# A hand-written instruction order for the attention start and the first block of layer 1, in place of the scheduler's

## The chip, the core and the metric

The program runs on one core of a Trainium2 chip. The metric is the device time of one execution in microseconds: the median of 3 runs of the kernel before is 971.0 (968.24 to 971.59). The profile comes from one further execution, which took 971.32 us; its recorded span, from the first to the last instruction, is 969.6 us. All times below count from the start of that span.

The engines are named as the profile names them: PE is TensorE (matmuls, PEld its weight loads), DVE is VectorE, ACT is ScalarE, POOL is GpSimd, SP is SyncE, which only issues DMAs here. ACT issues some DMAs too.

## The reference

Linear attention with a decaying state runs over 4 batches of 768 tokens with 8 heads of 48, and its output goes through two feed-forward layers (384 to 2048 and back):

```
state = alpha[:, :, t, :, None] * state + einsum(k[:, :, t], v[:, :, t])   # per head 48 x 48
y[:, :, t] = einsum(q[:, :, t], state)
x = y as (3072 tokens, 384)
h = x @ w_in;  g = max(0.01 * h, h);              x = g @ w_out            # layer 1
h = x @ w_in2; g = where(h > 0, h, exp(h) - 1);   out = g @ w_out2         # layer 2
```

The weights arrive as 64-bit floats, which the kernel converts itself.

## The kernel before

**Attention** is cut into 24 units of 128 tokens, all 8 heads together; six units are one batch, and the state goes from one unit to the next. Per unit u the work is this (the short names are used throughout):

- *prep*, DVE: a backward product scan E, two tiny ops for its end value (pe and its reciprocal), k times E (kS, in place in the packed input), a forward scan F, q times F (qh, in place).
- *sc*, PE: the scores, 16 instructions; *pk*, PE: kS transposed; *kn*, ACT: pk copied to SBUF.
- *mask*, DVE: two ops that make A from sc; *T*, DVE: the old state times pe.
- *po*, PE: A times v (16 instructions) and then T times qh (16 more); *pu*, PE: kn times v.
- *xh*, ACT: po to the high half of layer 1's input; *xl*, DVE: the low half; *S*, DVE: the new state from pu and T.
- After xh, ACT issues the loads of unit u + 3 (pack and v).

sc, pk, po and pu share three PSUM buffers in rotation, so pu(u) takes the place of po(u - 1) and waits until xl(u - 1) has read it. After the fourth unit of a block, six DMAs issued by SP (`gather`) move a part of the rows of x into place; only then can layer 1 of that block start.

**Layers.** A block is 4 units, 512 tokens. Step (j, m) of layer 1 takes block j and slice m of 16 of the hidden width: *h*, 9 matmuls on PE into hp; then *t* (ACT, 0.01 * hp), *max* (DVE), *gh* (ACT) and *gl* (DVE), which split g into two halves; *y*, 9 matmuls on PE that add into the block's output. Every product is made as three (high times high, low times high, high times low). Layer 2 has the same form, with other elementwise work.

**Conversions.** Slice m of layer 1's weights is needed from step (0, m) on. It is loaded into one of four staging tiles (`stage1`) and converted: two passes *p* on ACT, three ops *a* on DVE that depend one on another, *hi* on ACT, and the subtraction *b* on DVE. When b(m) is written, the load of slice m + 4 follows. So during attention's first units and block 0, DVE has three kinds of work: attention, conversions, and layer 1's max and gl. From block 1 on only two are left.

**What sets the order.** The program is written in some order, and a scheduler with its own model of the durations puts each engine's instructions in the order it finds best; each engine then runs its list strictly in that order, waiting at each instruction for what it needs. In the kernel before, only the first op of each conversion pass is pinned to its place in the program (`pin`). At the start come four whole units with two, then more conversions (`PC`), then block 0, whose steps carry the pieces of units 4 to 7 (`pieces`, one of attn_pe and attn_post each) and a conversion running ahead (`PS`). The scheduler is free to take later pieces earlier, and does.

Of the kernel before, what the change touches and what calls it, by code (L numbers as in the profile page):

```python
# [8 lines left out]
F32 = mybir.dt.float32  # L9
# [10 lines left out]
def attention_two_layers_kernel(  # L20
# [101 lines left out]
    def attn_prep(u):  # L122
# [3 lines left out]
        F = at_p.tile([PR, EXT], F32, tag="F", name="F")  # L126
# [5 lines left out]
        nc.vector.tensor_tensor_scan(F[:, 0:EXT - 1], t[:, 0:EXT - 1], d1[:, 0:EXT - 1], 0.0, ALU.mult, ALU.add)  # L132
        e2 = E[:, 1:EXT].rearrange("p (g c) -> p g c", c=C + 1)
        nc.vector.tensor_mul(kS, kS, e2[:, :, 1:C + 1])
        nc.vector.tensor_mul(qh, qh, ext(F, 0)[:, :, 1:C + 1])
        st[u] = dict(kS=kS, qh=qh, pe=pe)

    def attn_S(u):
        c = u % NC
        d = st[u]  # L140
        kS, qh = d["kS"], d["qh"]
        A = at_p.tile([128, 2, NP, C], F32, tag="A", name="A")
# [5 lines left out]
        d["A"], d["sc"] = A, sc  # L148
        if c < NC - 1:
            pk = ps_a.tile([128, NP, PR], F32, tag="at", name="pk")  # L150
            for p in range(NP):
                nc.tensor.transpose(pk[:, p, :], kS[:, p, :], ident[:PR, :PR])
            d["pk"] = pk

    def attn_S_post(u):
        c = u % NC
        d = st[u]
        for j, sc in enumerate(d.pop("sc")):
            nc.vector.tensor_mul(d["A"][:, j], sc, causal.unsqueeze(1).to_broadcast([128, NP, C]))
        if c < NC - 1:  # L160
# [3 lines left out]
        if c > 0:  # L164
            T = at_p.tile([PR, NP, D], F32, tag="cT", name="T")
            nc.vector.tensor_mul(T, st["S"], d["pe"].to_broadcast([PR, NP, D]))
            d["T"] = T

    def attn_V(u):
        c = u % NC  # L170
        d = st[u]
        vt = vts.pop(u)
# [13 lines left out]
        d["po"] = po  # L186
        if c < NC - 1:
# [9 lines left out]
    def attn_V_post(u, xh, xl, off):  # L197
        c = u % NC
        d = st.pop(u)
        po = d["po"]  # L200
        nc.scalar.copy(xh[0:PR, :, off:off + C], po)
        nc.vector.tensor_sub(xl[0:PR, :, off:off + C], po, xh[0:PR, :, off:off + C].bitcast(F32))
        if c < NC - 1:
            pu = d["pu"]
            Sn = at_p.tile([PR, NP, D], F32, tag="S", name="S")
            if c > 0:
                nc.vector.tensor_add(Sn, pu, d["T"])
            else:
# [11 lines left out]
    pinned = [False]  # L220

    def pin(ins):
        if pinned[0]:
            tc.keep_in_program_order(ins)

    def convert_p(raw, tp, ts, hi, lo):
        words = raw.rearrange("p (f t) -> p f t", t=2)
        rest = raw.bitcast(U16).rearrange("p (f t) -> p f t", t=4)[:, :, 1]
        pin(nc.scalar.activation(tp.bitcast(F32), words[:, :, 1].bitcast(F32), ACTF.Copy, scale=2.0 ** -112))
        nc.scalar.activation(words[:, :, 0], rest, ACTF.Copy, scale=2.0 ** -13)  # L230

# [27 lines left out]

    def ffn1_g(j, m):  # L260
        n = xt[j][2]
        hp = steps[1, j, m]
        t = g_p.tile([128, n], F32, tag="t", name="t")
        nc.scalar.activation(t, hp, ACTF.Copy, scale=0.01)  # L264
        nc.vector.tensor_max(t, t, hp)  # L265
        gh = gs_p.tile([128, n], F32R, tag="gh", name="gh")
        gl = gs_p.tile([128, n], F32R, tag="gl", name="gl")
        split(gh, gl, t, nc.scalar, nc.vector)
        steps[1, j, m] = gh, gl
# [303 lines left out]

    with ExitStack():
# [15 lines left out]
        LA = 2  # L590

        def conv_to(upto):
            pinned[0] = True
            for i in range(conv1.done[1], min(upto, len(order1))):
                conv1.a(i + 1)
                conv1.b(i + 1)
            pinned[0] = False

        attn_prep(0)
        for u in range(4):  # L600
            attn_pe(u, 0)
            attn_post(u, 1)
            attn_post(u, 0)
            attn_pe(u, 2)
            attn_post(u, 2)
            conv_to(PC[u] // 2)
# [9 lines left out]

        pieces = [(u, i) for u in range(4, NU) for i in range(4)]
        conv_to(LA)
        for s in range(LA):
            pe_h(seq[s])  # L620
            post_h(seq[s])
        for s, e in enumerate(seq):
            ph, j, m = e
            n = seq[s + LA] if s + LA < len(seq) else None
            now = []
            if ph == 1 and pieces:
# [34 lines left out]
            if ph == 2 and m >= KF - 10 and m % 2 == 0:  # L661
# [93 lines left out]
```

## Time and profile before

| what | value |
|---|---|
| median of 3 runs | 971.0 us |
| profiled execution | 971.32 us, span 969.6 us |
| PE busy | 929.8 us (96%), 5234 instructions |
| DVE busy | 529.4 us (55%) |
| ACT busy | 445.8 us (46%) |
| DMA | 62.38 MB, 64 GB/s on average, 243 GB/s in the first fortieth of the span |

The busy share is an average over unlike stages. From about 200 us on PE is never idle; DVE is the full engine between about 100 and 160 us, where attention, conversions and layer 1 come together; in the first 60 us no engine is full and DMA is at its busiest. A matmul counts as busy from its start to its modelled end, so a PE that is always busy may still do its work at half pace: there its instructions are longer.

### The profile page before, as it was taken

The page shows a single profiled execution, that of the slowest core. Times are in us where ns is not written, and L with a number is a line of the kernel's source. Part 1 is how long each engine was busy: PE and PEld are TensorE (multiplying, and loading weights), DVE is VectorE, ACT ScalarE, POOL GpSimd, SP SyncE. Part 2 cuts the span into 40 slices and gives each one's busy share as a digit, 9 for nine tenths or more (in the row PEclk, how much of TensorE's full clock was granted, in tenths as well). Part 3 has the DMA queues.
Part 4 walks back from the last instruction along what each step waited for, and adds up shares of the span by engine and source line. Part 5 has one row for each costly group of instructions (what it writes and reads, how often), then busy time and mean ns, then how long its engine had stood idle before and what let it go on. Part 6 is the DMA issues. An engine that isn't in the chain of part 4 may idle for free.

```text
span 969.6 us, 13094 instructions
## 1 busy us (share of the span) xinstructions
PE 929.8 (96%) x5234; PEld 781.8 (81%) x5234; DVE 529.4 (55%) x876; ACT 445.8 (46%) x783; POOL 1.1 (0%) x8
## 2 busy tenths in 40 slices
PE   4679999999999999999999999999999999999996
PEld 3557667887888788788878889999999999999995
DVE  6788998534555557454469983433433333333332
ACT  1344545322322323233367795574664744744442
POOL 0000000000000000000000000000000000000000
PEclk9969999999999999999999999999999999999998
DMA  9655561102111221211234330020100200100001
GB/s 243 184 152 160 153 181 45 29 13 58 42 41 41 58 71 53 58 41 50 58 96 141 115 98 10 1 81 1 62 20 1 72 10 1 62 0 1 33 1 37
DMA packets 25093, 62.38 MB, mean 64 GB/s; under 512 B 3936, under 2 KB 7008, under 8 KB 25024
## 3 DMA queue, kind: packets, MB, share of 16 engines
q1 hardware_dynamic: 19184, 40.54, 15.1%
q10 hardware_dynamic: 5840, 20.92, 7.5%
q8 instruction: 43, 0.70, 0.3%
q14 instruction: 26, 0.21, 0.1%
HBM read 54.37 MB, written 4.72 MB: 61 GB/s over the span
## 4 chain that ended last, share of the span: by engine, by line
PE 79%; DVE 8%; DMA 8%; ACT 2%; issue 1%; SPq 1%; DVEq 0%; ACTq 0%
PE hp L310 20%; PE hp L256 16%; PE y L281 15%; PE o L341 10%; PE oa L341 10%; DMA x2t<-in_w_dram 3%; DMA pack<-in_seqs_dram 2%; PE po L178 2%; DMA stg<-in_w_dram 2%; PE sc L147 2%; PE po L184 2%; DMA x<-x 1%; DVE x2t L235 1%; DVE t L265 1%; DVE gl L81 1%
## 5 line engine op out<-in xcount | busy, mean ns | idle before, releaser
L256 PE MATMUL hp<-x,w 128*128 128x512 f32 x864 | 218.6, 395 | 4.1 <-DMA x<-x 2.7
L310 PE MATMUL hp<-x,w 128*128 128x512 f32 x864 | 215.4, 393 | 0.0
L81 DVE TENSOR_TENSOR gl<-t,gh 128x512 fp32r<-128x512 f32 x192 | 132.7, 691 | 126.3 <-ACT gh L78 122.4
L78 ACT CAST gh<-t 128x512 fp32r<-128x512 f32 x192 | 119.0, 620 | 174.1 <-PE y L281 63.9
L256 PEld LDWEIGHTS hp<-x,w 128*128 128x128 f32 x864 | 160.4, 188 | 41.2 <-issue 3.2
L310 PEld LDWEIGHTS hp<-x,w 128*128 128x128 f32 x864 | 160.7, 188 | 29.3
L281 PE MATMUL y<-gh,w 128*128 128x512 f32 x576 | 173.2, 397 | 1.6 <-ACT gh L78 1.6
L319 DVE SCALAR_TENSOR_TENSOR t<-t,hp 128x512 f32<-128x512 f32 x96 | 66.0, 687 | 148.8 <-ACT t L318 148.8
L281 PEld LDWEIGHTS y<-gh,w 128*128 128x128 f32 x576 | 105.5, 188 | 25.6 <-ACT gh L78 3.0
L265 DVE TENSOR_TENSOR t<-t,hp 128x512 f32<-128x512 f32 x96 | 65.4, 683 | 73.8 <-ACT t L264 73.7
L281 PE MATMUL y<-gl,w 128*128 128x512 f32 x288 | 105.3, 394 | 0.0
L317 ACT ACTIVATE t<-hp 128x512 f32<-128x512 f32 x96 | 57.1, 595 | 103.7 <-PE hp L310 103.6
L264 ACT ACTIVATE t<-hp 128x512 f32<-128x512 f32 x96 | 56.8, 594 | 99.2 <-PE hp L256 99.2
L341 PE MATMUL oa<-w,gh 128*128 128x384 f32 x384 | 96.7, 337 | 0.0
L341 PE MATMUL o<-w,gh 128*128 128x384 f32 x384 | 94.7, 337 | 0.2 <-ACT x2t L292 0.2
L341 PEld LDWEIGHTS o<-w,gh 128*128 128x128 f32 x384 | 70.5, 188 | 6.0 <-ACT x2t L292 0.5
L341 PEld LDWEIGHTS oa<-w,gh 128*128 128x128 f32 x384 | 70.2, 188 | 2.9
L281 PEld LDWEIGHTS y<-gl,w 128*128 128x128 f32 x288 | 53.5, 188 | 12.1 <-issue 0.7
L341 PE MATMUL oa<-w,gl 128*128 128x384 f32 x192 | 63.0, 337 | 0.0
L318 ACT ACTIVATE t<-t 128x512 f32<-128x512 f32 x96 | 60.8, 633 | 2.3
L341 PE MATMUL o<-w,gl 128*128 128x384 f32 x192 | 61.0, 336 | 0.0
L147 PEld LDWEIGHTS sc<-pack 48*128 48x128 f32 x384 | 32.0, 210 | 20.3 <-issue 9.3
(89 smaller groups left out, 761.5 us busy)
## 6 DMA issues: line engine op xcount, KB each, us to landing
pack<-in_seqs_dram ACTq DMA_DIRECT2D x21, 674.2 KB, 4.8
stg<-in_w_dram SPq DMA_DIRECT2D x28, 384.0 KB, 3.4
x2t<-in_w_dram SPq DMA_DIRECT2D x20, 384.0 KB, 4.3
vt<-in_vals_dram ACTq DMA_DIRECT2D x21, 288.0 KB, 3.0
span<-in_seqs_dram SPq DMA_DIRECT2D x24, 226.2 KB, 2.7
x2t<-in_w_dram SPq DMA_DIRECT2D x32, 144.0 KB, 3.6
out_dram<-osb SPq DMA_DIRECT2D x24, 192.0 KB, 2.1
x<-x SPq DMA_DIRECT2D x36, 64.0 KB, 4.4
```

The costliest lines, as they stand in the source:

```text
L78: nc.scalar.copy(dst, src)
L81: (lo_engine or nc.vector).tensor_sub(lo, src, dst.bitcast(F32))
L147: nc.tensor.matmul(sc[j][:, p], lhsT=kS[r, p, :], rhs=qh[r, p, :], start=True, stop=True)
L256: nc.tensor.matmul(hp, lhsT=a[:, kk, :], rhs=x[:, kk, :n], start=(i == 0), stop=(i == 3 * KD - 1))
L264: nc.scalar.activation(t, hp, ACTF.Copy, scale=0.01)
L265: nc.vector.tensor_max(t, t, hp)
L281: nc.tensor.matmul(ytiles[j][c], lhsT=a[:, c * 128:(c + 1) * 128], rhs=x, start=(m == 0 and i == 0), stop=(m == KF - 1 and i == 2),)
L310: nc.tensor.matmul(hp, lhsT=a[:, kk, :], rhs=x[:, kk, :], start=(i == 0), stop=(i == 3 * KD - 1))
L317: nc.scalar.activation(t, hp, ACTF.Relu, scale=-1.0)
L318: nc.scalar.activation(t, t, ACTF.Exp, scale=-1.0)
L319: nc.vector.scalar_tensor_tensor(out=t, in0=t, scalar=-1.0, in1=hp, op0=ALU.add, op1=ALU.max)
L341: nc.tensor.matmul(otiles[j][i], lhsT=a[:, i * 128:(i + 1) * 128], rhs=x, start=(m == 0 and n == 0), stop=(m == KF - 1 and n == 2),)
```

## The change

Every function of a unit is split into its single operations, and these are written in a new order. `quarter(u, i)` holds unit u's second half together with unit u + 1's first half:

```diff
+        def quarter(u, i, chain=True):
+            if i == 0:
+                attn_pu(u)
+                prep_k(u + 1)
+                attn_T(u)
+            elif i == 1:
+                attn_mask(u)
+                if chain:
+                    attn_pk(u + 1)
+                    attn_kn(u + 1)
+                attn_po(u)
+            elif i == 2:
+                prep_F(u + 1)
+                attn_state(u)
+                prep_q(u + 1)
+                if chain:
+                    attn_sc(u + 1)
+                attn_xh(u, xh, off)
+                next_load(u + 3)
+            else:
+                attn_xl(u, xh, xl, off)
...
+                    gather(t, blocks[j][1] * C)
```

Conversions 0 to 2 and the first two steps of layer 1 are placed by hand between the quarters of units 2 to 4, and block 0's loop places one conversion and at most one quarter per step:

```diff
+        for u in range(UB):
+            for i in range(3):
+                quarter(u, i)
+            if u > 1:
+                conv1.a(u - 1)
+            quarter(u, 3)
+            if u > 1:
+                conv1.b(u - 1)
+            if u > 0:
+                conv1.p(u)
...
+            if s < KF:
+                ffn1_y(j, m)
+                pe_h(n)
+                ffn1_t(n[1], n[2])
+                conv1.a(s + 4)
+                if s < KF - LA:
+                    for p in quarters[13 * s // (KF - LA):13 * (s + 1) // (KF - LA)]:
+                        quarter(*p, chain=p[0] + 1 < UB + blocks[1][1])
+                ffn1_max(n[1], n[2])
+                ffn1_gh(n[1], n[2])
+                conv1.b(s + 4)
+                ffn1_gl(n[1], n[2])
+                conv1.p(s + 5)
+                in_order()
+                continue
```

`in_order` ties every instruction up to there to the one before it on its engine, so that the scheduler keeps the written order; `behind` ties all later instructions behind the last of these, and the rest of the program is scheduled as before:

```diff
+    def in_order():
...
+            if i >= traced[0] and y is not None:
+                tc.add_manual_dep(
+                    x, y.name,
+                    mybir.DependencyInfo(mybir.DependencyClass.NoSync, mybir.DependencyReason.DATA),
+                    reason="in_order")
...
-    pinned = [False]
-
-    def pin(ins):
-        if pinned[0]:
-            tc.keep_in_program_order(ins)
```

The first loads are reordered on SP's queue:

```diff
         constants()
+        load_unit(1)
         load_v(0)
-        load_unit(1)
+        load_unit(2)
+        load_v(1)
         stage1(0)
-        load_v(1)
-        stage1(1)
-        load_unit(2)
         load_v(2)
-        stage1(2)
-        stage1(3)
+        for m in range(1, 4):
+            stage1(m)
```

What this makes of DVE's list in unit 2, where the first conversion stands. Before, from unit 2's second mask (L159) on; L128 to L135 are the prep of unit 3, L234, L235, L237 and L241 are conversion 0 (a, a, a, b), L202 is xl(2):

```order
L159 TENSOR_TENSOR A<-sc_253,causal 128x512
L130 TENSOR_SCALAR pe<-E 112x4
L134 TENSOR_TENSOR pack<-pack,E 112x512
L131 RECIPROCAL d_97<-pe 112x4
L132 SCALAR_TENSOR_TENSOR F<-pack,d_97 112x516
L207 TENSOR_TENSOR S<-pu,T 112x192
L234 TENSOR_SCALAR x2t_138<-x2t_134 128x768
L135 TENSOR_TENSOR pack<-pack,F 112x512
L235 SCALAR_TENSOR_TENSOR x2t_138<-x2t_138 128x768
L166 TENSOR_TENSOR T<-S,pe 112x192
L237 ISA x2t_138<-x2t_134,x2t_138 128x1536
L202 TENSOR_TENSOR x<-po,x 112x4x128
```

And now (L180 mask of unit 2, L139 and L144 the rest of prep 3, L248 S, L275 to L278 conversion 0's a, L240 xl(2), L282 its b):

```order
L180 TENSOR_TENSOR A<-sc_317,causal 128x512
L180 TENSOR_TENSOR A<-sc_318,causal 128x512
L139 SCALAR_TENSOR_TENSOR F<-pack,d_97 112x516
L248 TENSOR_TENSOR S<-pu,T 112x192
L144 TENSOR_TENSOR pack<-pack,F 112x512
L275 TENSOR_SCALAR x2t_138<-x2t_134 128x768
L276 SCALAR_TENSOR_TENSOR x2t_138<-x2t_138 128x768
L278 ISA x2t_138<-x2t_134,x2t_138 128x1536
L240 TENSOR_TENSOR x<-po,x 112x4x128
L282 TENSOR_TENSOR w_0_103<-x2t_138,w_0_102 128x768
```

The two masks now stand together, and conversion 0's three dependent ops stand one right behind the other, where before an op of the attention stood between each two.

On PE, at the start of layer 1. Before, from the first matmul of unit 4's po on: one matmul of h(0, 0) and one of h(0, 1) (L256) stand inside unit 4's attention:

```order
L152 MATMUL pk<-ident,pack 128x112 x4
L178 MATMUL po<-A,vt 64x128
L256 MATMUL hp<-x,w_0_102 128x512
L256 MATMUL hp<-x,w_1_104 128x512
L192 MATMUL pu<-vt,kn 64x48
```

And now, from the end of unit 4's pu on (L231): all of h(0, 0) (L297), then unit 4's po (L212):

```order
L231 MATMUL pu<-vt,kn 48x48
L297 MATMUL hp<-x,w_0_102 128x512 x3
L297 MATMUL hp<-x,w_0_103 128x512 x3
L297 MATMUL hp<-x,w_0_102 128x512 x3
L212 MATMUL po<-A,vt 64x128
```

The steps of layer 1 are whole now, and h(0, 0) stands ahead of unit 4's po.

In block 0's loop, DVE's list for step s = 2 (a of conversion 5, the prep of unit 6 and T, max of step 4, b of conversion 5, gl of step 4):

```order
L275 TENSOR_SCALAR x2t_139<-x2t_135 128x768
L276 SCALAR_TENSOR_TENSOR x2t_139<-x2t_139 128x768
L278 ISA x2t_139<-x2t_135,x2t_139 128x1536
L127 SCALAR_TENSOR_TENSOR E<-pack,d_96 112x517
L129 TENSOR_SCALAR pe<-E 112x4
L130 RECIPROCAL d_97<-pe 112x4
L132 TENSOR_TENSOR pack<-pack,E 112x512
L187 TENSOR_TENSOR T<-S,pe 112x192
L308 TENSOR_TENSOR t<-t,hp 128x512
L282 TENSOR_TENSOR w_5_113<-x2t_139,w_5_112 128x768
L318 TENSOR_TENSOR gl<-t,gh 128x512
```

Every one of the steps s = 0 to 12 has this form, with another quarter, or none, in the middle; before, two conversions at a time were open in this stretch and mixed with two units' attention.

## Rows read from the trace of the kernel before

**Rows 1.** Windows: stretch, its length, busy us (instructions) by engine, PE clock, DMA.
```profile
0.00:61.00 61.00, 34.59 (x278) 27.84 (x278) 46.24 (x78) 17.29 (x23) 1.08 (x8) 0.88 0.75 199
74.20:177.80 103.60, 100.43 (x632) 74.38 (x633) 91.04 (x142) 50.04 (x77) 0.00 (x0) 1.00 0.46 129
177.80:250.00 72.20, 72.20 (x369) 57.92 (x370) 33.06 (x53) 21.50 (x36) 0.00 (x0) 1.00 0.09 24
```

**Rows 2.** Waits of PE: waiting line, releaser, us in total, times, longest.
```profile
PE po L178 <- DVE A L159: 9.5, 7, 2.7
...
PE pk L152 <- DVE x L202: 6.0, 4, 2.8
```

**Rows 3.** Windows of line L147 (sc) alone, up to 177.8 us.
```profile
0.00:177.80 177.80, 21.68 (x176) 18.21 (x176) 0.94 0.57 157
```

**Rows 4.** Windows of line L256 (h of layer 1) alone, up to 177.8 us.
```profile
0.00:177.80 177.80, 46.90 (x171) 30.96 (x171) 0.94 0.57 157
```

**Rows 5.** Timeline of PE: start, length, line, operation [idle before, releaser].
```profile
8.88 2.08 PE L147 MATMUL sc<-pack 48*128 48x128 f32 x16 [8.88 <-DVE pack L135]
...
40.84 1.95 PE L184 MATMUL po<-pack,T 48*48 48x128 f32 x16
...
42.71 1.19 PE L147 MATMUL sc<-pack 48*128 48x128 f32 x16
...
61.19 1.19 PE L256 MATMUL hp<-x,w 128*128 128x512 f32 x2 [1.88 <-DMA x<-x]
...
97.20 0.55 PE L152 MATMUL pk<-ident,pack 112*128 112x112 f32 x4
...
102.35 0.67 PE L192 MATMUL pu<-vt,kn 128*64 128x48 f32 x16
...
200.79 2.20 PE L256 MATMUL hp<-x,w 128*128 128x512 f32 x9
...
204.87 2.20 PE L256 MATMUL hp<-x,w 128*128 128x512 f32 x9
...
229.25 1.09 PE L178 MATMUL po<-A,vt 128*64 128x128 f32 x16
230.27 1.08 PE L184 MATMUL po<-pack,T 48*48 48x128 f32 x16
```

**Rows 6.** Timeline of DVE.
```profile
55.56 0.69 DVE L202 TENSOR_TENSOR x<-po,x 112x512 fp32r<-112x512 f32 x1
...
87.05 0.56 DVE L234 TENSOR_SCALAR x2t<-x2t 128x768 int32<-128x768 int32 x1
87.71 0.96 DVE L235 SCALAR_TENSOR_TENSOR x2t<-x2t 128x768 int32<-128x768 int32 x1
88.71 0.96 DVE L237 CUSTOM_DVE_ANT_0 x2t<-x2t,x2t 128x1536 uint16<-128x1536 uint16 x1
...
124.00 1.24 DVE L128 TENSOR_TENSOR_SCAN E<-pack,d 112x517 f32<-112x517 f32 x1
...
128.78 0.55 DVE L234 TENSOR_SCALAR x2t<-x2t 128x768 int32<-128x768 int32 x1
...
132.65 0.35 DVE L166 TENSOR_TENSOR T<-S,pe 112x192 f32<-112x192 f32 x1
132.92 0.95 DVE L237 CUSTOM_DVE_ANT_0 x2t<-x2t,x2t 128x1536 uint16<-128x1536 uint16 x1
133.78 0.68 DVE L265 TENSOR_TENSOR t<-t,hp 128x512 f32<-128x512 f32 x1
134.38 0.69 DVE L135 TENSOR_TENSOR pack<-pack,F 112x512 f32<-112x512 f32 x1
```

**Rows 7.** Timeline of ACT.
```profile
12.29 1.28 ACT L230 ACT_TABLE_LOAD   x1 [12.29 <-DMA x2t<-in_w_dram]
...
54.10 0.58 ACT L201 CAST x<-po 112x512 fp32r<-112x512 f32 x1 [0.59 <-PE po L184]
```

**Rows 8.** Chain of waits in order of time: start, length, what.
```profile
15.30 9.64 DMA pack<-in_seqs_dram
```

More of the change, by code (lines that the diff above doesn't have):

```diff
@@ L186, in attn_V, with attn_pu @@
         d["po"] = po
+    def attn_pu(u):
+        c = u % NC
+        d = st[u]
+        vt = vts[u]
         if c < NC - 1:
@@ L258, in ffn1_h, with ffn1_t, ffn1_max, ffn1_gh @@
         steps[1, j, m] = hp
-    def ffn1_g(j, m):
[L261 to L269, printed above, removed]
+    def ffn1_t(j, m):
+        t = g_p.tile([128, xt[j][2]], F32, tag="t", name="t")
+        nc.scalar.activation(t, steps[1, j, m], ACTF.Copy, scale=0.01)
+        steps[1, j, m] = t, steps[1, j, m]
+    def ffn1_max(j, m):
+        t, hp = steps[1, j, m]
+        nc.vector.tensor_max(t, t, hp)
+    def ffn1_gh(j, m):
+        gh = gs_p.tile([128, xt[j][2]], F32R, tag="gh", name="gh")
+        nc.scalar.copy(gh, steps[1, j, m][0])
+        steps[1, j, m] = steps[1, j, m][0], gh
+    def ffn1_gl(j, m):
+        t, gh = steps[1, j, m]
+        gl = gs_p.tile([128, xt[j][2]], F32R, tag="gl", name="gl")
+        nc.vector.tensor_sub(gl, t, gh.bitcast(F32))
+        steps[1, j, m] = gh, gl
+    def ffn1_g(j, m):
+        for f in (ffn1_t, ffn1_max, ffn1_gh, ffn1_gl):
+            f(j, m)
     ytiles = {}
@@ L572, in general, with behind @@
                 ffn2_y(j, m)
+    traced = [0]
+    def in_order():
+        ins = list(nc.cur_bb.bb.instructions)
+        last = {}
+        for i, x in enumerate(ins):
+            y = last.get(x.engine)
+            if i >= traced[0] and y is not None:
[3 more added lines that the diff above has]
+                    reason="in_order")
+            last[x.engine] = x
+        traced[0] = len(ins)
+    def behind():
+        ins = list(nc.cur_bb.bb.instructions)
+        last = {x.engine: x for x in ins[:traced[0]]}
+        for x in ins[traced[0]:]:
+            if x.engine in last:
+                tc.add_manual_dep(
+                    x, last[x.engine].name,
+                    mybir.DependencyInfo(mybir.DependencyClass.NoSync, mybir.DependencyReason.DATA),
+                    reason="behind")
     with ExitStack():
@@ L590, in attention_two_layers_kernel @@
         LA = 2
[L592 to L597, printed above, removed]
-        attn_prep(0)
[L600 to L606, printed above, removed]
+        UB = blocks[0][1]
+        def quarter(u, i, chain=True):
+            j = unit_block[u]
+            xh, xl, _, t = xtile(j)
+            off = (u - blocks[j][0]) * C
+            if i == 0:
+                attn_pu(u)
+                prep_k(u + 1)
+                attn_T(u)
+            elif i == 1:
+                attn_mask(u)
+                if chain:
+                    attn_pk(u + 1)
+                    attn_kn(u + 1)
+                attn_po(u)
+            elif i == 2:
+                prep_F(u + 1)
+                attn_state(u)
+                prep_q(u + 1)
+                if chain:
+                    attn_sc(u + 1)
+                attn_xh(u, xh, off)
+                next_load(u + 3)
+            else:
+                attn_xl(u, xh, xl, off)
+                st.pop(u)
+                if u == blocks[j][0] + blocks[j][1] - 1:
+                    gather(t, blocks[j][1] * C)
+        attn_prep(0)
+        attn_sc(0)
+        attn_pk(0)
+        attn_kn(0)
+        for u in range(UB):
[8 more added lines that the diff above has]
+                conv1.p(u)
+        conv1.a(UB - 1)
+        quarter(UB, 0)
+        ffn1_h(0, 0)
+        ffn1_t(0, 0)
+        quarter(UB, 1)
+        conv1.b(UB - 1)
+        ffn1_max(0, 0)
+        ffn1_gh(0, 0)
+        quarter(UB, 2)
+        ffn1_h(0, 1)
+        ffn1_t(0, 1)
+        ffn1_gl(0, 0)
+        conv1.p(UB)
+        ffn1_max(0, 1)
+        ffn1_gh(0, 1)
+        ffn1_gl(0, 1)
+        in_order()
         seq = [(1, j, m) for j in range(NB) for m in range(KF)]
@@ L615, in post_h @@
             (ffn1_g if e[0] == 1 else ffn2_g)(e[1], e[2])
[L617 to L621, printed above, removed]
+        quarters = [(u, i) for u in range(UB, UB + blocks[1][1]) for i in range(4)][3:]
+        pieces = [(u, i) for u in range(UB + blocks[1][1], NU) for i in range(4)]
         for s, e in enumerate(seq):
@@ L668, in attention_two_layers_kernel @@
                     guard()
+        behind()
         with tc.If(nc.values_load(near, min_val=0, max_val=1) == 0):
```

83 lines of the change are left out of this document (52 added, 31 removed).

## The prediction

> **What bounds the kernel now.** I read the windows by stage first. In the last of the three stretches shown PE is busy for all of its 72.2 us [rows 1]; from there on the end moves with PE's work, and 969.6 - 177.8 = 791.8 us of span follow. In the first 61 us neither PE (34.6) nor DVE (46.2) is full; from 74.2 to 177.8 PE is busy for 100.4 of 103.6 [rows 1]. The waits of PE come next: po for the masks 9.5 us, pk for xl 6.0 us (its PSUM place) [rows 2]. [...] So the yardstick is: what had PE done by a given time, and what does the rest cost at full pace. By 177.8 us sc of 176 / 16 = 11 units was done [rows 3], seven more than the four that block 0 needs, and 171 matmuls of h [rows 4].
>
> **The change, part by part.** It adds and removes no arithmetic; it moves it. Three terms decide: when block 0's loop starts, how long DVE needs for it, and how much less attention is done by its end.
>
> Prices on DVE, start to next start (or length less the overlap of 0.08 that max shows, 0.68 long and followed after 0.60) [rows 6]: a scan 1.15, an op on 512 columns (mask, kS, qh, xl, max, gl) 0.60, T or S 0.27, a conversion's ops 0.47, 0.87, 0.87, and b 0.87 like L237, which has the same columns. pe and its reciprocal I put at 0.1 each, an estimate below T's 0.27. A unit is 2 x 1.15 + 5 x 0.60 + 2 x 0.27 + 0.2 = 6.0.
>
> The hand order puts dependent ops back to back. Where that happens before, L234 to L235 takes 0.66 and L235 to L237 1.00 [rows 6]; a conversion then costs 0.66 + 1.00 + 0.87 + 0.87 = 3.40, not 3.08. [...]
>
> *To the loop.* sc(0) starts at 8.88 us [rows 5]. DVE's work from there to the loop: preps of units 1 to 5, 5 x 3.7 = 18.5; masks of units 0 to 4, 6.0; nine of S and T, 2.4; xl of 0 to 3, 2.4; conversions 0 to 2, 10.2; max and gl of two steps, 2.4. Sum 41.9, so without a wait 50.8. Waits, with PE at full pace or at half:
> - Unit 0: the table load (1.28 [rows 7]) stands ahead of the first kn, since ACT's list begins with it and it took its successor's wait before. pu(0), pk(1) and po(0) queue behind kn(0), and behind them S(0) and xl(0) on DVE, all at half pace: I walk 1.6 + 2.9 = 4.5.
> - Unit 1: after the masks DVE has F, S and qh, 2.0 us; xl(1) waits for the rest of pk 0.5, po and T 2.0 or 4.1, xh 0.58 [rows 5, 7] and three hops of about 0.07: 1.3 or 3.4.
> - Units 2 and 3: a conversion's a (2.5) fills that gap, and hi stands behind xh and two DMA issues on ACT: 0.4 or 3.5 for both.
> - The end: behind qh(5) come sc(5) 1.1, h(0, 1) 2.04 and t (about 0.6, as xh), less gl's 0.6: 3.2; then gh(0, 1) stands behind two conversion passes on ACT: 1.2 more, or 1.7.
>
> Full pace 10.6, so 61.4; half 16.3, so 67.1. The first unit is at half pace and the long stretches po, T, sc can raise the clock as they did at 42.71 [rows 5]; I take the middle, 64.3. Loads hide this only if pack(3) lands: before it took 9.64 us from its issue [rows 8]; issued at about 18.8 (behind xh(0)) it lands at 28.4, about when E(3) comes up. The gather's six DMAs end 61.19 - 56.25 = 4.9 us after xl [rows 5, 6]; conversion 2 and the prep of unit 5 cover that on DVE.
>
> *The loop*, steps 0 to 12 on DVE: 13 x (3.40 + 1.20) = 59.8; attention 17.6 (xl(4) 0.6, units 5 and 6 5.8 each, unit 7 without xl 5.4): 77.4. PE has 13 steps of 204.87 - 200.79 = 4.08, 53.0, and some 11 us of attention [rows 5]: 64, so DVE is the bound and PE waits. Waits of DVE: after b, h's last six matmuls (1.5), t and hops make 2.2, gl and the next a 3.1, so nothing in a plain step. After a mask, PE's po and T (2.15 with hops), y and h (4.08), t and hops (0.8) make 7.0 to the next max, while DVE has max, b, gl, a, F, S and qh, 6.6; after a qh, sc in place of po and T makes 5.9 against DVE's 5.2 (max, b, gl, a, xl). Twice each, with hi's 0.45 in step 0: 3 us. The loads of the staged weights follow b by SP three steps ahead of their p, some 18 us against the 9.64 of the slowest landing shown [rows 8], and cost nothing unless they land twice as late; then ACT's p, and DVE's a behind it, wait for the rest. Step 13 starts at 64.3 + 77.4 + 3 = 144.7. xl(7) 0.6, gather 4.9, then h(1, 0), y(0, 15) and h(1, 1) of 2.04 each: 156.3. PE idles some 3 us of that for the gather, with nothing else in its list to fill it.
>
> *What is owed.* At that point units 0 to 7 are done and 18 steps of h (162 matmuls); the kernel before had by 177.8 units 8, 9 and 10 as well. Each is sc 1.1, pk 0.55, po 1.02, T 1.0, pu 0.67 = 4.35 [rows 5], 13.0 in all, and 9 matmuls of 4.08 / 18 = 0.227, 2.0: 15.0 us.
>
> Sum: 156.3 + 15.0 + 791.8 = 963.1 of span. The profiled execution lies 1.7 above its span (971.3 to 969.6): 964.8, say **965**. That execution is 0.3 above the median of 971.0, so it stands for it. From block 1 on the order is the scheduler's again, and PE is full in both; I cost that at nothing, and at up to 1 us for each idle gap it leaves.
>
> Bounds, by the same steps: low, full pace, conversions at 3.08 and no wait in the loop: 61.4 + 73.2 = 134.6, then 146.2, and 954.7 at the end. High, 67.1 and a wait of 1 us in each of 13 steps: 157.5, then 169.1, and 977.6. The sum stands between them, nearer the low one because the quarters give DVE something to do while PE catches up.
>
> **The rivals.**
> - *B, DVE never waits.* The low bound, 955. For it: half pace gives way to full after the long stretch po, T, sc at 42.71 [rows 5], and conversions cover units 2 and 3. [...] Against: PE at half pace for most of 8.88 to 42.
> - *C, the round trip sets the step: slower.* Place: block 0's loop, where max(s + 2) stands in DVE's list behind h(s + 2), which needs b(s + 2) of the step before, and two passes on ACT stand ahead of t. I leave 0.9 us of slack in a plain step. If the true trip is longer than DVE's work between, everything behind max waits, 13 times. From 0.5 us a step (13 x 0.5 = 6.5) the gain is gone; at 1 us to 1.2 us it is 978 to 980. For it: PE at half pace would need 1.4 more for the six matmuls alone, and no other work of DVE may pass max now. Against: a quarter stands in twelve of the 13 steps, and PE is at full pace in the like stretch before (clock 1.00) [rows 1].
> - *D, the gain is eaten.* Half pace to the loop (2.8 later) and packs late by some 3.5 us, since all the staged weights share the DMA engines with pack(3): 971, no change. For it: DMA landing took 9.64 [rows 8]; against: packs 1 and 2 now go ahead of the weights.
> - *That the order is not what it says* is excluded: the listing shows DVE and PE in the written order.
>
> **How the numbers follow.** My forecast (960 to 970) 0.50, B 0.20, D 0.14, C 0.16. What a measurement can tell from no change is 0.5%, so faster means below 966.1 and slower above 975.9. Faster: 0.29 of the forecast's 0.50 and all of B, 0.20, with 0.01 of D: 0.50. Slower: C but for 0.01, 0.15. Same: 0.35. The range, 954 to 977, takes in B's and most of C's time and leaves about 0.2 outside.
>
> **What would show it.** Right: y(0, 0) starts at 58 to 64 us, when before h(0, 0) had only begun (61.19 [rows 5]); from there to about 144 DVE is busy nearly throughout and PE is not; dependent conversion ops start 0.66 and 1.00 apart; an idle PE of 2 to 3 us before h(1, 0), released by the gather; block 1 takes about 83 us (16 x 4.08 + 4 x 4.35), not the 72 of before. Wrong: PE's rows at full pace from unit 1 on (B); DVE idle ahead of max in every step (C); E(3) or p released by a DMA (D); idle gaps of PE after block 0.

## The result, and the profile after

The changed kernel takes 976.8 us (median of 5 runs, 975.9 to 979.5) against 971.0: 1.0072 times the time before, 95% interval 1.005 to 1.0095. It is slower by 0.7%, where 965, a gain, was forecast; it lies just inside the stated range of 954 to 977, near the time of rival C. Its profiled execution took 976.15, span 974.4 us.

The windows of the changed kernel, columns as in [rows 1]:

```profile
0.00:61.00 61.00, 34.42 (x317) 27.20 (x317) 43.88 (x76) 14.27 (x20) 1.14 (x8) 0.78 0.83 209
...
0.00:75.00 75.00, 46.68 (x390) 36.67 (x391) 52.46 (x88) 21.17 (x31) 1.14 (x8) 0.82 0.73 188
...
70.00:155.84 85.84, 72.76 (x386) 55.15 (x385) 76.80 (x110) 47.57 (x68) 0.00 (x0) 0.92 0.39 113
...
74.20:177.80 103.60, 88.93 (x458) 67.60 (x458) 83.70 (x123) 52.73 (x78) 0.00 (x0) 0.92 0.38 107
177.80:250.00 72.20, 72.20 (x485) 57.50 (x484) 44.93 (x74) 19.17 (x32) 0.00 (x0) 1.00 0.22 61
```

In the stretch from 74.2 to 177.8, where PE was busy for 100.4 us at a granted clock of 1.00 [rows 1], it is now busy for 88.9 at 0.92. From 177.8 on it is full, as before. A window of the kernel before, to set beside the second row, and its first y:

```profile
0.00:75.00 75.00, 48.40 (x370) 37.84 (x371) 58.21 (x98) 24.96 (x35) 1.08 (x8) 0.86 0.73 195
...
74.48 1.52 PE L281 MATMUL y<-gh,w 128*128 128x512 f32 x6
```

By 75 us DVE, which the forecast had as the bound of the loop, had worked 58.2 us before and has worked 52.5 now. The first y comes 8.0 us earlier (66.49, before 74.48), but with 3 conversions behind it instead of 4 and the three ops a of a fifth. So far the earlier y is DVE work put off, not saved.

PE's timeline after (start, length, line, operation, idle before and releaser); L158 is sc, L166 pk, L212 and L218 po and T, L297 h, L335 y:

```profile
33.23 1.01 PE L166 MATMUL pk<-ident,pack 112*128 112x112 f32 x4 [4.64 <-DVE A L180]
...
54.95 4.77 PE L297 MATMUL hp<-x,w 128*128 128x512 f32 x9 [5.15 <-DMA x<-x]
...
66.49 0.62 PE L335 MATMUL y<-gh,w 128*128 128x512 f32 x2
...
86.87 2.09 PE L297 MATMUL hp<-x,w 128*128 128x512 f32 x6 [2.05 <-DVE w L282]
88.75 0.95 PE L166 MATMUL pk<-ident,pack 112*128 112x112 f32 x4
90.79 2.45 PE L212 MATMUL po<-A,vt 128*64 128x128 f32 x16 [1.09 <-DVE A L180]
...
159.68 0.47 PE L297 MATMUL hp<-x,w 128*128 128x512 f32 x1 [0.68 <-DMA x<-x]
160.99 0.47 PE L297 MATMUL hp<-x,w 128*128 128x512 f32 x1 [0.84 <-DMA x<-x]
162.21 2.66 PE L297 MATMUL hp<-x,w 128*128 128x512 f32 x7 [0.76 <-DMA x<-x]
...
167.55 2.21 PE L297 MATMUL hp<-x,w 128*128 128x512 f32 x9
```

Three places lose time. h(0, 0) waits 5.15 us for the gather and then runs at half pace (4.77 for nine matmuls that take 2.2 at 167.55; the granted clock is 0.50 there and 1.00 at 167.55). In the loop PE waits for b (2.05 at 86.87), and the next pk and po run at about half pace (0.95 and 2.45, in [rows 5] 0.55 and 1.09; granted clock 0.50 from 88.75 to 93.2). At the edge to block 1 h(1, 0) dribbles, released piece by piece by the gather.

DVE's timeline after:

```profile
26.23 0.69 DVE L240 TENSOR_TENSOR x<-po,x 112x512 fp32r<-112x512 f32 x1 [2.92 <-ACT x L237]
30.08 1.23 DVE L127 TENSOR_TENSOR_SCAN E<-pack,d 112x517 f32<-112x517 f32 x1 [3.15 <-DMA pack<-in_seqs_dram]
...
60.38 0.69 DVE L308 TENSOR_TENSOR t<-t,hp 128x512 f32<-128x512 f32 x1 [2.95 <-ACT t L303]
...
67.32 0.69 DVE L308 TENSOR_TENSOR t<-t,hp 128x512 f32<-128x512 f32 x1 [3.65 <-ACT t L303]
69.39 0.69 DVE L318 TENSOR_TENSOR gl<-t,gh 128x512 fp32r<-128x512 f32 x1 [1.39 <-ACT gh L312]
70.00 0.55 DVE L275 TENSOR_SCALAR x2t<-x2t 128x768 int32<-128x768 int32 x1
...
80.21 0.56 DVE L275 TENSOR_SCALAR x2t<-x2t 128x768 int32<-128x768 int32 x1
80.87 0.96 DVE L276 SCALAR_TENSOR_TENSOR x2t<-x2t 128x768 int32<-128x768 int32 x1
81.97 0.96 DVE L278 CUSTOM_DVE_ANT_0 x2t<-x2t,x2t 128x1536 uint16<-128x1536 uint16 x1
...
99.96 0.69 DVE L308 TENSOR_TENSOR t<-t,hp 128x512 f32<-128x512 f32 x1 [2.15 <-ACT t L303]
```

The loop's first DVE op stands at 70.00. ACT's timeline after; L237 is xh(0), L111 issues pack(3), L173 is kn(1), and the last two rows begin the copies that close blocks 0 and 1:

```profile
16.41 0.58 ACT L237 CAST x<-po 112x512 fp32r<-112x512 f32 x1 [1.31 <-PE po L212]
21.88 0.32 ACTq L111 DMA_DIRECT2D pack<-in_seqs_dram  x1
...
22.88 0.53 ACT L173 COPY kn<-pk 128x448 f32<-128x448 f32 x1 [5.88 <-DMA x2t<-in_w_dram]
...
167.75 0.59 ACT L346 COPY x2t<-y 128x512 f32<-128x512 f32 x1 [0.38 <-PE y L335]
...
254.79 0.58 ACT L346 COPY x2t<-y 128x512 f32<-128x512 f32 x1 [0.68 <-PE y L335]
```

ACT stands for 5.88 us, DMA issues within, before kn(1); 4.9 of it lie between the end of xh(0), 16.99, and the issue. E(3) on DVE then waits 3.15 us for that pack. Block 1 takes 87.0 us, before 71.7 (176.09 to 247.82).

### The profile page after: what moved, and what is told of

The parts are those of the page before. It is cut to its first block, busy times and chain, and to the rows that moved or that the text cites. A ratio compares the mean times of both kernels' runs of the same rounds, so it can differ in the third digit from the quotient of the medians.

```text
span 974.4 us, 13128 instructions
## 1 busy us (share of the span) xinstructions
PE 922.9 (95%) x5234; PEld 779.2 (80%) x5234; DVE 532.4 (55%) x876; ACT 445.9 (46%) x783; POOL 1.1 (0%) x8
## 4 chain that ended last, share of the span: by engine, by line
PE 84%; DVE 6%; DMA 6%; issue 1%; SPq 1%; ACT 1%; DVEq 0%; ACTq 0%
PE hp L364 21%; PE y L335 18%; PE hp L297 18%; PE oa L395 10%; PE o L395 10%; DMA x2t<-in_w_dram 2%; PE sc L158 2%; PE po L212 2%; PE po L218 2%; DMA vt<-in_vals_dram 2%; DVE x2t L276 1%; DVE x2t L278 1%; DMA pack<-in_seqs_dram 1%; DMA x<-x 1%; DVE x2t L275 1%
## 5 line engine op out<-in xcount | busy, mean ns | idle before, releaser
L297 PE MATMUL hp<-x,w 128*128 128x512 f32 x864 | 219.6, 397 | 14.8 <-DMA x<-x 7.4
L297 PEld LDWEIGHTS hp<-x,w 128*128 128x128 f32 x864 | 162.2, 190 | 54.3 <-DVE w L282 8.0
L335 PE MATMUL y<-gh,w 128*128 128x512 f32 x576 | 179.8, 400 | 0.0
L335 PEld LDWEIGHTS y<-gh,w 128*128 128x128 f32 x576 | 106.9, 191 | 23.5 <-issue 1.1
L335 PE MATMUL y<-gl,w 128*128 128x512 f32 x288 | 109.9, 395 | 0.0
L335 PEld LDWEIGHTS y<-gl,w 128*128 128x128 f32 x288 | 54.5, 189 | 12.1
```

What stands on the lines that cost most here:

```text
L297: nc.tensor.matmul(hp, lhsT=a[:, kk, :], rhs=x[:, kk, :n], start=(i == 0), stop=(i == 3 * KD - 1))
L335: nc.tensor.matmul(ytiles[j][c], lhsT=a[:, c * 128:(c + 1) * 128], rhs=x, start=(m == 0 and i == 0), stop=(m == KF - 1 and i == 2),)
```

## The experiments

A time in brackets is the range of a kernel's runs, a ratio its time over the kernel before's with its 95% interval. The kernel before ran anew beside each group of experiments, with medians of 971.0 to 972.4; so medians of two groups can differ by 1.4 us without any change. "First y" and "block 0 ends" (start of the last row of its copies to x2t, which can hold two copies) are from the profiled execution. For the changed kernel they are 66.49 and 167.75.

**Which half loses?** loop_free drops the tie in the loop, start_free the tie of the start (`traced[0]` is set there, and nothing is tied).

```diff
                 conv1.p(s + 5)
-                in_order()          # loop_free
...
         ffn1_gl(0, 1)
-        in_order()                  # start_free
+        traced[0] = len(list(nc.cur_bb.bb.instructions))
```

> The hand order holds up to the first two steps of layer 1; block 0's loop is written as before in the same program order, but the scheduler may rearrange it. Theory 1 (the loop's order costs: the quarter stands ahead of max and b in DVE's list, so PE starves for b, drops to its lower clock and DVE then waits for PE): the loss is gone and the earlier start of layer 1 remains (first y at 66.5 us against 74.5 before), so 963 to 968 us. Rival, theory 2 (the start costs: half pace of PE and late loads before the loop): the loop is DVE-bound in either order, so no better than 972 to 977.

978.7 (977.0 to 980.8), ratio 1.0077 (1.0048 to 1.0106); first y 66.34, block 0 ends 184.18. Here the loop is left to the scheduler and only the start is by hand: slower than the kernel before, so the first theory fell. By 75 us this kernel has as many E (7), xl (5) and matmuls of h (27) as the kernel before, but 3 conversions and a part of two more, where the kernel before is at the last op of its fifth. Its DVE has worked 53.1 us by then, before 58.2. Up to there the hand-made start saves DVE nothing.

> The opposite part alone: the scheduler orders everything before block 0's loop, the loop keeps the hand order. Theory 1: the start was the part that gained, so this is as slow as the changed kernel or slower, 977 to 985 us. Theory 2: the start was the part that lost, so 966 to 972.

984.4 (982.2 to 987.8), ratio 1.0142 (1.0112 to 1.0171); first y 72.69. This is the first theory's time: for the new program the hand order of the start is worth 7.6 us. Where the scheduler orders it, E waits for packs:

```profile
DVE E L127 <- DMA pack<-in_seqs_dram: 10.7, 3, 5.0
```

So neither half alone is the one that loses: with either given back to the scheduler the new program is no faster than the changed kernel. No run gave it both halves, so what the new program and its order of the first loads cost apart from the ties is not shown.

**The gather and b.** early_gather puts one quarter into each of the first 13 steps, so that the last, and the gather behind it, come a step earlier. late_quarters puts a quarter's DVE ops behind gl and its PE and ACT ops into the next step, behind h and ahead of t.

```diff
-                    for p in quarters[13 * s // (KF - LA):13 * (s + 1) // (KF - LA)]:
+                    for p in quarters[s:s + 1]:        # early_gather
```

> Hand order throughout, but each quarter of block 0 one step earlier (steps 0 to 12 instead of 1 to 13), so that xl(7) and the gather for block 1 come a step earlier. If the edge of the blocks costs what the trace shows there (PE idle or in single matmuls between 159 and 162 us, about 2.3 us), 974 to 975 us. Theory 1 alone (waits inside the loop): no more than 1 us from 976.8, since the same quarters still stand ahead of max and b.

972.1 (970.7 to 974.3), ratio 1.001 (0.9995 to 1.0025): 4.7 below the changed kernel by the medians, more than expected, and 2.0 by the spans of the profiled executions (972.4 and 974.4). Block 0 ends at 165.14. PE's timeline at the edge:

```profile
160.75 2.48 PE L297 MATMUL hp<-x,w 128*128 128x512 f32 x9
165.11 2.20 PE L297 MATMUL hp<-x,w 128*128 128x512 f32 x9
```

h(1, 0) no longer waits, and h(1, 1) starts 2.4 earlier than at 167.55.

> Hand order throughout, same quarters in the same steps, but in each step DVE has a, max, b, gl first and the quarter's ops last, and PE's and ACT's part of a quarter stands in the next step behind h. Theory 1: PE no longer waits for b behind a prep or a mask (5.8 us of such waits in the changed kernel), stays at full pace through the loop, and DVE's waits for t go; the loop is 5 to 8 us shorter: 968 to 972 us. Theory 2: nothing before the loop changes, so 975 to 977.

979.2 (977.2 to 979.8), ratio 1.0079 (1.0055 to 1.0102). PE's waits for b are gone, but 10.3 us of waits for hi came in their place, since the quarter's copies now stand ahead of t and hi on ACT; and the gather came later (h(1, 0) waits 4.43 at 159.22). It mixed two things and settled nothing on b.

**On the round trip or off it.** Both kernels have one quarter a step, its DVE ops behind b; in the program quarter_lag has its PE and ACT ops at the head of the next step, ahead of y, quarter_behind_b right there. On PE both give the same order (h, pk, po, T, y, h), which is also that of early_gather.

```diff
+                if late:
+                    quarter_pe(*late.pop())            # quarter_lag
                 ffn1_y(j, m)
                 pe_h(n)
...
                 conv1.b(s + 4)
+                    for p in quarters[s:s + 1]:
+                        quarter_dve(*p)                # quarter_behind_b: quarter(*p)
```

> One quarter in each of the first thirteen steps, as in early_gather; its DVE ops stand behind b, and its PE and ACT ops (pu, pk, po, sc, kn, xh) stand at the head of the next step, ahead of y and so of t and hi. Theory R (the round trip b, h, t, max, b sets the loop, and the quarter ahead of b lengthens it): PE's waits for b (6.1 in early_gather) and those for the masks in the loop go, DVE's waits for t there fall below 8, first y stays at 66.2, block 0's last x2t copy starts at 160 to 163 (165.1 in early_gather), the time is 967 to 970. Rival W (DVE is near its work already; the waits only change place): other waits of the same sum appear, block 0 ends at 164 to 167, time 971 to 975.

1003.2 (1000.2 to 1003.9), ratio 1.0322 (1.0285 to 1.036). The expectation failed by 35 us, with the sign wrong. PE and DVE, one after the other:

```profile
86.73 2.45 PE L212 MATMUL po<-A,vt 128*64 128x128 f32 x16 [5.43 <-DVE A L180]
...
94.99 2.35 PE L297 MATMUL hp<-x,w 128*128 128x512 f32 x9
...
98.01 0.69 DVE L308 TENSOR_TENSOR t<-t,hp 128x512 f32<-128x512 f32 x1 [7.60 <-ACT t L303]
```

po waits for the mask (behind b) and stands ahead of y and h, so po, T, y and h all lie between this b and the next max, po, T and y at half pace (granted clock 0.50 from 86.7 to 95). From b (85.03) to max (98.01) it takes 13.0 us, with little for DVE to do. From 60 to 185 us DVE waits 35.4 us for t, in early_gather 18.6. There the mask stands ahead of max and b, so PE does po while DVE does max, b and gl, and F and qh stand ahead of the next max: from b (86.32) to max (94.64) 8.3 us. That is C's mechanism at its full price.

> As early_gather, but with the whole quarter (its PE and ACT ops too) behind b and ahead of gl. Theory R: PE's waits for b go, but PE now stands at the end of its step for masks and qh that come later on DVE, so the waits for A rise by about what those for b lose; 970 to 974. Rival (only the place of b counts): 967 to 970, block 0 ends at 160 to 163.

1000.9 (998.2 to 1002.3), ratio 1.0292 (1.025 to 1.0334): DVE waits 34.5 us for t, by the same mechanism. Both theories fell; what decides is whether po, waiting for a mask behind b, stands on PE ahead of the next y and h.

**Loads.** loads_in_turn issues packs 3 to 6 on SP instead of ACT, with the staged weights 1 to 3 behind packs 3 to 5. packs_on_pool issues only those packs and their v from POOL and leaves the weights where they were.

```diff
-        for m in range(1, 4):
-            stage1(m)
...
+            if u < 3:
+                stage1(u + 1)                          # behind quarter(u, 2)
...
-            load_unit(u, eng=nc.scalar)
+            load_unit(u, eng=nc.sync if u < 7 else nc.scalar)   # load_v too; packs_on_pool: nc.gpsimd
```

> The changed kernel with the loads of the first units in the order of use: packs 3 to 6 and their vt on the SP queue instead of ACT's, and the staged weights 1, 2 and 3 behind pack 3, 4 and 5 on it. Theory L (ACT's list stood for DMA issues and the pack came late because the weights were ahead of it): DVE's 3.15 us for pack(3) and ACT's 5.9 ahead of kn(1) go, first y comes 3 to 4 us earlier, 62 to 64, time 972 to 974. Rival (16 DMA engines are busy 0.83 of the first 61 us anyway: the weights then come late instead): p and a wait by as much, first y at 66 to 67, time 976 to 978.

970.7 (969.0 to 973.1), ratio 0.9994 (0.9975 to 1.0014): 6.1 below the changed kernel. First y 64.14. Pack(3)'s issue and E(3):

```profile
12.14 0.33 SPq L111 DMA_DIRECT2D pack<-in_seqs_dram  x1
...
27.14 1.23 DVE L127 TENSOR_TENSOR_SCAN E<-pack,d 112x517 f32<-112x517 f32 x1
```

> Packs 3 to 6 and their vt issued from POOL's list, the weights as in the changed kernel. Tells the two halves of loads_in_turn apart. If ACT's list standing at the DMA issue was the cost: kn(1) starts at 21 to 22 instead of 22.88 and pack(3) is issued at 16.5 to 18 instead of 21.9, E(3) waits under 1, first y 64 to 65, time 971 to 973. If the weights ahead of the pack in the DMA engines were the cost: pack(3) takes longer from issue to landing (over 10 us), E(3) still waits 2 to 3, time 975 to 977.

973.5 (969.3 to 974.8), ratio 1.0009 (0.9995 to 1.0023); first y 64.06, block 0 ends 162.01.

```profile
12.35 0.67 POOL L111 DMA_DIRECT2D pack<-in_seqs_dram  x1 [10.46 <-PE pk L166]
...
27.05 1.23 DVE L127 TENSOR_TENSOR_SCAN E<-pack,d 112x517 f32<-112x517 f32 x1
```

The pack's buffer is free at 12.1 to 12.4. ACT issued the load 9.5 us later, behind xh(0) and a stand that the profile puts down to a load of weights. With the weights' loads untouched E(3)'s wait is gone too, and packs 3 to 5 land 7.9 us after their issue by the median, in the changed kernel 8.2; so the late issue from ACT's list is the cause of the wait, not the bytes ahead of the pack. Most of it is the stand: issued at 16.99, when xh(0) was done, and landing 8.2 later, by an estimate at 25.2, the pack would have been there before E(3)'s turn at 26.93. Why ACT stood is not shown; in fill_pe_wide below xh(0) ended at 19.17 and the pack was issued at 21.72 all the same. The medians leave up to 2.8 us that the weights' later place may add; the two profiles don't show it, and the intervals of the two ratios overlap.

**Both.** loads_and_gather is these two edits together, loads_in_turn's and early_gather's.

> The two edits that gained, together: loads in the order of use (loads_in_turn) and the quarters one step earlier each (early_gather). If the changed kernel loses at two separate places, at its loads before the loop and at the gather behind it, the gains add: 976.8 - 6.1 - 4.7 = 966, 965 to 968. If both save the same late half pace or the same wait (early_gather also moved the rest of the loop), less than 2 us come on top: 969 to 971.

966.2 (964.8 to 969.1), ratio 0.9943 (0.9926 to 0.996): the gains add, 976.8 - 6.1 - 4.7 = 966.0. That it fits to 0.2 us is chance: by the ratios the two gains are 0.8% and 0.6%, both together 1.3%. This is faster than both kernels. First y 63.80, block 0 ends 159.25.

**b once more, with the loads in turn.** lag_behind_hi is late_quarters with the loads in turn, the quarter's ACT ops behind t and hi, and one quarter a step (its PE ops stand behind h, as there); lag_two has two quarters in its first step.

```diff
                 conv1.a(s + 4)
...
+                if late:
+                    quarter_pe(*late.pop())            # lag_two: all of late
...
                 ffn1_gl(n[1], n[2])
+                    for p in quarters[s:s + 1]:        # lag_two: quarters[s + (s > 0):s + 2]
+                        quarter_dve(*p)
+                        late.append(p)
```

> loads_in_turn, one quarter a step, with a quarter's DVE ops at the end of its step and its PE ops behind h of the next, its ACT ops behind hi there (late_quarters had them ahead of t and hi; quarter_lag had the PE ops ahead of y). Theory R' (what counts is that nothing of a quarter stands on the trip b, y, h, t, max): no waits of PE for masks or b in the loop, DVE's waits for t below 6 there, block 0's last x2t copy at 157 to 160, time 962 to 966. Rival (the chain of quarters itself, mask to pk, kn, pu, T, gets one step longer each and the gather later): no better than loads_and_gather, 967 to 974, PE waiting for sc's qh or for the gather at the edge.

970.4 (969.4 to 972.8), ratio 0.9985 (0.9972 to 0.9997): the rival. PE waits for hi (11.5 us), and for the gather at the edge (2.4).

> lag_behind_hi with two quarters in its first step, so that the last quarter, and the gather behind it, come one step earlier. If lag_behind_hi lost its gain at the edge only (its PE idled 149 to 160 for hi and the gather): block 0's last x2t copy starts at 157 to 160 (162.8 there) and the time is 964 to 967, at or below loads_and_gather's 966.2. If the loop itself is no shorter because DVE has its work there anyway: 968 to 971, with PE's waits for hi (11.5) still there.

967.5 (965.5 to 967.8), ratio 0.9954 (0.9936 to 0.9971). The time lies between the two forecasts. The gather's wait at the edge is gone, and about 3 us with it. The loop itself, first y to the end of block 0, is 161.01 - 64.97 = 96.0 us, in loads_and_gather 95.5. PE's wait has only changed its name:

```profile
PE hp L297 <- ACT w L279: 13.2, 8, 3.4
```

In loads_and_gather PE waits 6.0 us for b and 4.1 for masks. From 75 to 150 us DVE works 68.5 us here and 68.2 there. So taking the quarter from ahead of b gained nothing: DVE has its work there, and PE waits for it under one name or another. Whether it would gain with hi in time, no run shows.

**PE's pace.** Three kernels fill PE's gaps before the loop with products of a constant that nothing uses.

```diff
+                nc.tensor.matmul(wps, lhsT=d0[:, 0:128].bitcast(F32R), rhs=d0[:, 0:512].bitcast(F32R), start=True, stop=True)
...                                   # fill_pe: f32, rhs=d0[:, 128:192]
+                if i == 0:
+                    warm((0, 5, 10, 10)[u])            # all_three; and warm(16) ahead of ffn1_h(0, 0)
```

> The changed kernel with matmuls added that compute nothing of use (128x64 products of a constant into a PSUM tile that y uses later): 24 ahead of sc(0), 12 behind each pu of units 0 to 3, 30 behind pu(4), where PE stands idle. Theory P (PE's half pace is what delays DVE up to the loop): granted clock in 8.8 to 55 rises from 0.76 to over 0.9, po and T of units 1 and 2 take 1.0 to 1.1 instead of 1.95, DVE's waits for xh (2.5, 2.9) fall by 1.5 or more each, h(0, 0) takes 2.1 instead of 4.8, first y comes 3 to 6 us earlier (60 to 63) and the time is 971 to 974. Rival (packs and the gather hold the start, not the pace): E(3) waits longer for its pack by what is gained before, first y moves by under 1.5 us but for h(0, 0)'s 2.5, and the time stays within 2 us of 976.8.

985.7 (981.2 to 990.2), ratio 1.0125 (1.0079 to 1.0171). A blunder of size: each product ran as two instructions, so the fillers delayed sc(0) and h (first y 79.88), and the pace did not rise for good:

```profile
1.67 10.50 PE L703 MATMUL warm<-d 112*128 112x64 f32 x48 [1.67 <-DVE d L92]
12.10 2.08 PE L158 MATMUL sc<-pack 48*128 48x128 f32 x16
...
27.23 2.89 PE L703 MATMUL warm<-d 112*128 112x64 f32 x24
...
56.12 13.06 PE L703 MATMUL warm<-d 112*128 112x64 f32 x60
```

After 10.5 us without a gap sc still takes 2.08, half pace. The fillers behind pu(1) ran at full pace (2.89 for 24, behind pu(0) 5.38), and units 1 and 2 with them (po and T 1.1); those behind pu(4) at half pace again (13.06 for 60), and h(0, 0) behind them took 4.19. So this run says little on theory P.

> As fill_pe, with fewer and wider products (128x512, one pass each): 8 ahead of sc(0), 4 behind each pu of units 0 to 3, 9 behind pu(4). fill_pe's 128x64 took 0.22 each in two passes, twice what its places held, and the pace stayed at half. Theory P (PE's half pace delays DVE up to the loop): if these rows raise the pace, po and T of units 1 to 3 take 1.0 to 1.1, h(0, 0) 2.1, and first y comes 2 to 4 us earlier than 66.5, time 972 to 975. Rival (pace is not what holds the start): po at 1.0 and first y still at 65.5 to 66.5. If the pace stays at half although PE is busy, the run says nothing on P, and first y moves later by what the fillers delay, under 3 us.

974.9 (972.5 to 977.7), ratio 1.0035 (1.0018 to 1.0051). PE's and then DVE's timeline:

```profile
20.54 1.20 PE L703 MATMUL warm<-d 112*128 112x512 f32 x4
22.95 0.61 PE L166 MATMUL pk<-ident,pack 112*128 112x112 f32 x4 [1.22 <-DVE A L180]
23.55 1.09 PE L212 MATMUL po<-A,vt 128*64 128x128 f32 x16
...
29.95 1.24 DVE L127 TENSOR_TENSOR_SCAN E<-pack,d 112x517 f32<-112x517 f32 x1 [2.94 <-DMA pack<-in_seqs_dram]
```

For unit 1 the pace was full (1.09, not 1.97), yet E(3) starts at 29.95, in the changed kernel at 30.08: what the pace gave was lost to pack(3). For units 2 and 3 it was at half again (po 1.97 at 34.04 and 44.66), and from 8.8 to 55 us the granted clock was 0.75 on average, without fillers 0.76. So on theory P as a whole the run says little; first y came at 65.87, 0.6 earlier.

> loads_and_gather with wide products that compute nothing of use in PE's gaps before the loop: 5 behind pu(1), 10 behind pu(2) and pu(3), 16 ahead of h(0, 0), none behind pu(0). If half pace is a cost of its own once the packs are in time: pk, po and T of units 2 and 3 at 0.6, 1.1 and 1.1, h(0, 0) about 2 instead of 4.3, DVE's wait for xh(1) stays at 2.9 or falls, first y at 59 to 62 (63.8 in loads_and_gather), time 962 to 964.5. If the masks and the gather hold PE anyway: first y within 0.8 us of 63.8 but for h(0, 0)'s 2, time 965 to 967.

965.5 (963.1 to 966.6), ratio 0.9934 (0.9916 to 0.9952). loads_and_gather with fillers: first y came as the first theory said, at 61.08, 2.7 earlier, though h(0, 0) still took 3.83 for its last eight matmuls (at 50.49). The time did not: block 0 ends at 159.68, there at 159.25. Windows of loads_and_gather, then of all_three:

```profile
75.00:100.00 25.00, 20.59 (x116) 15.67 (x115) 21.97 (x33) 14.01 (x21) 0.00 (x0) 0.93 0.54 151
100.00:125.00 25.00, 21.09 (x121) 16.11 (x120) 22.74 (x33) 14.18 (x21) 0.00 (x0) 0.93 0.56 156
125.00:150.00 25.00, 20.34 (x121) 15.33 (x119) 23.45 (x35) 14.54 (x21) 0.00 (x0) 1.00 0.24 66
```

```profile
75.00:100.00 25.00, 21.66 (x121) 16.73 (x123) 20.36 (x28) 13.98 (x21) 0.00 (x0) 0.86 0.53 147
100.00:125.00 25.00, 20.97 (x121) 16.41 (x117) 23.17 (x34) 14.62 (x22) 0.00 (x0) 0.93 0.56 161
125.00:150.00 25.00, 21.22 (x116) 15.91 (x114) 21.80 (x32) 12.79 (x19) 0.00 (x0) 0.86 0.19 54
```

The loop gave it back: in the same 75 us PE's clock was lower (0.86 twice), and DVE worked 65.3 us, there 68.2; by 150 us it has worked the same in both (123.2 and 123.3). DVE's waits from the end of h(0, 0) to 155 us, in loads_and_gather (from 63) and in all_three (from 61), say the same:

```profile
DVE t L308 <- ACT t L303: 9.1, 5, 3.6
```

```profile
DVE t L308 <- ACT t L303: 11.8, 5, 3.7
```

It waits 2.7 us more for t, as much as the start had won. That half pace in the loop is the reason is what these windows suggest; no run held the pace up in the loop, so it is not shown.

## Why the prediction was wrong

The span came out 974.4, forecast 963.1: 11.3 too little, and the change lost where it was to gain. The steps that failed are the waits up to the loop, the trip within it, and the edge, each walked with PE faster or a load earlier than they were. By the forecast's own steps:

- **What bounds**: right, DVE. Its chained ops were dearer still than forecast: a conversion's start 0.66, 1.10 and 0.88 apart (80.21 to 82.85), forecast 0.66, 1.00 and 0.87. The half pace of PE before 43 us (T 1.95 at 40.84, 1.08 at 230.27 [rows 5]) was read off lengths; the profile's granted clock reads 1.00 there, and no run shows why the two differ.
- **To the loop, 64.3: measured 70.00, 5.7 too little.** That is later than even the 67.1 for half pace. Of the 61.2 from sc(0) on DVE waited 17.4, forecast 13.4 (the middle), and the rest is 43.8, forecast 41.9. The waits of units 0 to 3, apart from the pack, were 6.2, some 2.6 less than the middle, which hid a part of two larger misses. Two sentences failed. "Issued at about 18.8 ... it lands at 28.4, about when E(3) comes up": it was issued at 21.88, and E(3) waited 3.15. I had seen ACT's list stand behind kn(0) but not ahead of the DMA issue, where it stood from 16.99 on. And at the end, forecast 4.4 to 4.9, it was 2.95 + 3.65 + 1.39 = 8.0: PE stood for the gather and then did h(0, 0) at half pace. "Conversion 2 and the prep of unit 5 cover that on DVE" held for the gather alone, not for h behind it.
- **The loop, 80.4: measured 85.84 (70.00 to 155.84), 5.4 too little.** Half of it is work: 85.84 less DVE's waits of 5.6 is 80.2, forecast 77.4, since chained ops start later than I priced them: the third of a conversion 1.10 behind the second (in 12 of 13, priced 1.00), kS 1.56 behind E (three times, priced 1.35), and b and gl behind a max that waited. The other half is waits, 5.6 where I took 3: 2.15 at 99.96, 1.12 at 126.15, 2.02 at 153.51, and 0.3. I walked the trip after a mask at full pace; PE waited for b in the steps with a prep, and the po behind it ran at half pace or near it (2.45, 1.87 and 1.58). This is rival C's mechanism, in three steps of 13 and not in all.
- **The edge: 13.9, forecast 11.6.** From xl(7) at 155.84 to the end of h(1, 1), 167.55 + 2.21 = 169.8. The gather was walked; that h and y behind it run below full pace (2.66 for seven matmuls of h, 2.21 for nine at 167.55; granted clock 0.65 from 162.2 to 164.9, then 0.70 to 167.5) was not.
- **Owed, 15.0**: 974.4 - 169.8 - 791.8 = 12.8, so 2.2 too much.

Together 5.7 + 5.4 + 2.3 - 2.2 = 11.2. Rival D had named the late pack and the half pace, but for the start alone, and with 971. C had the direction and the mechanism and came nearest in time, but by a wait in each step; the misses at the start and the edge are not in it, so that it came near is in part luck. B's condition, full pace, did not come; the low bound was never near. Block 1 took 87.0, forecast 83.

The forecast's way of adding up did hold. In all fourteen kernels with the hand-made loop the span ends 805.0 to 809.5 us after block 0 does (974.4 - 167.75 = 806.7 in the changed kernel); in the two whose loop is the scheduler's it ends 793.5 (before) and 791.3 (loop_free) after. So the attention owed costs some 13 us, and block 0 has to end that much earlier for the change to break even. It ended 8.3 earlier, in loads_and_gather 16.8.

Behind the sizes stands one omission. The forecast valued an early loop against what PE had done before by 177.8 us, and never set DVE's work by 75 us in both kernels side by side. The kernel before had 58.2 us done (46.2 of it by 61 us [rows 1]), the hand order 52.5: DVE waits longer in it. That comparison would have warned, but it doesn't settle the time: loads_and_gather has 55.1 us done by then, still less than the kernel before, and is faster.

Two edits to what DVE and PE wait for, the loads (6.1) and the gather (4.7), take the changed kernel to 966.2. That this is near the forecast's 965 is chance, since neither edit was in the change. Taking the quarter from ahead of b gained nothing that can be measured. Quickening PE's start brought 1.9 us by the medians alone (fill_pe_wide; the intervals of the two ratios just touch) and 0.7 on top of the two edits (all_three), which the runs do not tell from nothing.

## What to carry to other kernels

Where one engine is the bound, compare its busy time up to one and the same moment in both kernels before counting an earlier start of the next stage as a gain; less work done by then is a warning, not yet a loss. A DMA issue in the list of an engine that computes was reached here at 16.99 and started at 21.88, while its buffer was free at 12.1 to 12.4; look for a queue whose list is free then. In a hand-made pipeline, walk each step's round trip at PE's half pace as well as at full (nine matmuls of h took 4.77 and 2.21 here), and let no op that has long to wait stand ahead of it on the same engine (from b to max it took 13.0 us in quarter_lag, 8.3 in early_gather).

## What the hardware showed

In fill_pe PE was busy without a gap from 47 to 68 us, with fillers and attention, and the granted clock was 0.50 all that time:

```profile
47.00:68.00 21.00, 21.00 (x132) 19.69 (x131) 13.40 (x20) 4.41 (x6) 0.00 (x0) 0.50 0.60 150
```

From 27 to 43 us the same kind of fillers had run at a granted clock of 1.00. PE's busy time alone did not tell here which clock was granted. The forecast's middle of 64.3 took it that the long stretches po, T, sc can raise the clock, an estimate from one place, 42.71 [rows 5]. In the changed kernel sc behind po and T took 1.16 at 37.37 and 47.45 but 2.08 at 25.50; what raises the clock no run shows.

A second thing to know when reading these profiles: at the start of these runs the clock column and the lengths can differ. In fill_pe it reads 1.00 from 2 to 15 us, yet sc takes 2.08 at 12.10 and 1.16 at 76.62; in the changed kernel it reads 0.98 from 8.8 to 20 us, yet sc takes 2.08 at 8.81 and 1.16 at 16.29.
